# Float32 rows for two blocks of the weight fold, joint group scores, accumulating transfers last in the local sums, and a new instruction order

## The chip, the cores and the metric

The kernel runs on one core of a Trainium2 chip. The metric is the device time of that core in microseconds, the median of three runs. TensorE (PE) multiplies matrices, VectorE (DVE) and ScalarE (ACT) work element by element, GpSimd (POOL) and SyncE (SP) mostly start transfers.

## The reference

Attention over q, k, v of 8 batches x 8 heads x 576 positions x 64, the sum of two parts, and then a gated feed-forward block over all 4608 tokens:

```python
q_d = q.reshape(B, H, Sd, 4, D).mean(axis=3)          # k_d, v_d alike: pooled by 4
out_up = np.repeat(sm_attn(q_d, k_d, v_d), 4, axis=2)  # pooled attention, repeated
mask = np.abs(pos[:, None] - pos[None, :]) < 4         # each position and 3 to either side
out_local = softmax(where(mask, q @ k.T / 8, -1e9)) @ v
x = (out_up + out_local)  ->  (4608, 512)
h = ((x @ w1) * (x @ w2)) @ w3;   out = h @ w_out      # 512->1024, 1024->1024, 1024->512
```

The weights arrive as 64-bit words. The output is float32.

## The kernel before

**Stages.** The two last weight matrices are multiplied first (the fold: w3 @ w_out, 1024 x 512, kept in `wphl`). Then each chunk `c` of 384 tokens (twelve of them, `moe`) runs eight "gates" steps (x @ w1 and x @ w2, product in `a`, split into `gh` and `gl`) and "down" products with the folded weight. A product in full precision is three float32r matmuls (function `three`, lines 312 to 314): each operand is split into a high and a low part, and high x high, high x low, low x high are added up in PSUM.

**The fold.** Its inner dimension is cut into eight blocks `j`, its rows into eight blocks `m` (`mq` 0 has m = 0 to 3, `mq` 1 the others), so 64 products, each three matmuls of 512 columns. For a block `j`, a row block of w_out and one of w3 are loaded as 64-bit words (`words`), put together into float32 on ACT and DVE (`rebase`, `low`, and `join` on line 359), and split (`parted`): ACT casts the high part (line 371), DVE subtracts it for the low part (line 375). Four raw buffers hold loads (`early_raw`). Before the products PE runs 20 matmuls of zeros (`warm`, line 412).

**Attention.** In batches 0 and 1 (`PB`) the local part is computed by PE: `pooled_sums` loads q (`q4`, one transfer for each pair of heads) and k (`k4`), turns q (`qn`, line 672) and adds up four positions each for the pooled attention (`qks`); `group_scores` makes scores of 16 positions against 18 (line 769), two of its calls (`qd` 0 and 1) for each of six units; DVE adds the mask `band` and takes maxima, ACT exponentiates. In batches 2 to 7 (18 units, `unit`) DVE and ACT compute it: seven products q x shifted k, their sums, a softmax over seven, and seven products `pv` with the shifted v. These are added into `xl` in a fixed sequence, of which the places in `dma_add` are accumulating transfers started by POOL (line 958) and the others are additions on DVE (line 960). DVE then transposes (line 964), adds the pooled part (line 971), ACT and DVE split the result into `xh` and `xl` of the chunk (line 978). `quad` is the pooled attention.

**What sets the order.** All steps are tasks of a planner. A table of numbers (`ORDER`) gives each engine its tasks in a fixed sequence; every engine works strictly in that sequence and waits for semaphores where data or a buffer is not there yet. Buffer counts stand in `BUFS`.

Of the kernel before, what the change touches and what calls it, by code (L numbers as in the profile page):

```python
# [20 lines left out]
FAC = 4  # L21
# [31 lines left out]
            g=2, o=2, ab=2, acc=1, ps=3, p=1, pt=1, oup=2, vs=1, qks=1, x=2, s=3, gs=3, q4=2, k4=2, qn=2, vw=4, se=4, pte=1, xf=1)  # L53


SHARE = dict(qk_pool=(), qk_act=(2, 4), av_act=(3, 5), dma_add=(2, 4, 6))
TOKENS = 2
WARM = 20
# [94 lines left out]
    ),  # L153
    Pool=(
# [3 lines left out]
    ),  # L158
    SP=(
# [1064 lines left out]
```

## Time and profile before

| | |
|---|---|
| median of 3 runs | 749.47 us (749.1 to 751.64) |
| profiled execution, span | 747.4 us |
| its own time outside the span | not recorded; the median stands 2.1 us over the span |
| PE busy | 729.4 us (98%) |
| DVE busy | 617.8 us (83%), from 200 to 600 us 95% |
| ACT busy | 544.3 us (73%) |
| POOL busy | 108.2 us (14%) |
| chain that ended last | PE 96%, DVE 2%, DMA 1% |

A matmul's record is longer than its share of time, since the next one starts before it ends; spacing from start to start is what counts. A float32 matmul is two records, one of float32r is one.

### The profile page before, as it was taken

Reading aid. Unit: us, or ns where it says so; the run is one execution under the profiler, and the core shown is the slowest. Engines: PE = TensorE matmul, PEld = TensorE weight load, DVE = VectorE, ACT = ScalarE, POOL = GpSimd, SP = SyncE. Lnnn points to the kernel's source line nnn. Section 1 sums busy time; section 2 is a strip of 40 time slices with the busy share of each in tenths; the row PEclk is TensorE's granted clock in tenths of the full one; section 3 lists DMA queues with packets and bytes.
Section 4 is the critical chain, followed back from the end, with each engine's and each line's share of the span. In section 5 each row is a group of like instructions: output and inputs, shape, how many; then the busy total and the mean of one; then the engine's idle time right before and its main releaser. Section 6 shows DMA issues by size and latency. Waiting matters only on the chain.

```text
span 747.4 us, 15049 instructions
## 1 busy us (share of the span) xinstructions
PE 729.4 (98%) x5352; PEld 658.2 (88%) x5352; DVE 617.8 (83%) x1088; ACT 544.3 (73%) x2157; POOL 108.2 (14%) x139
## 2 busy tenths in 40 slices
PE   4999999999999999999999999999999999999997
PEld 3677888789998989999898998999899999999996
DVE  6988996557999999989999998999989988885212
ACT  5999878566897878778878886877887875853211
POOL 2020002210112210212222110221120110010000
PEclk9999999999999999999999999999999999999999
DMA  8998765746767877396577674668666354233101
GB/s 257 322 261 262 236 204 105 131 84 194 151 143 175 167 171 189 61 241 165 89 168 220 120 184 150 100 197 176 141 145 164 63 152 127 63 66 56 43 0 43
DMA packets 51999, 111.91 MB, mean 150 GB/s; under 512 B 5060, under 2 KB 19396, under 8 KB 51924
## 3 DMA queue, kind: packets, MB, share of 16 engines
q0 software_dynamic: 14592, 38.94, 30.9%
q1 hardware_dynamic: 37044, 71.74, 29.0%
q8 instruction: 42, 0.69, 0.4%
q10 hardware_dynamic: 288, 0.27, 0.1%
q14 instruction: 33, 0.27, 0.1%
HBM read 80.26 MB, written 9.44 MB: 120 GB/s over the span
## 4 chain that ended last, share of the span: by engine, by line
PE 96%; DVE 2%; DMA 1%; issue 0%; ACT 0%; SPq 0%
PE pab L312 19%; PE pab L314 18%; PE pab L313 18%; PE acc L312 9%; PE acc L313 9%; PE acc L314 9%; PE o_ps L553 2%; PE accw L312 2%; PE s_ps L592 2%; PE t_ps L631 2%; PE accw L313 2%; PE accw L314 2%; PE se_ps L769 1%; PE oe_ps L812 1%; PE te_ps L739 1%; DMA q<-in_qk_dram 1%
## 5 line engine op out<-in xcount | busy, mean ns | idle before, releaser
L942 ACT ACTIVATE pv<-kv,s 128x64 f32<-128x64 f32 x432 | 115.3, 338 | 15.2 <-DVE s L919 8.9
L894 ACT ACTIVATE junk<-pr 128x64 f32<-128x64 f32 x432 | 110.2, 255 | 17.3 <-DVE pr L884 8.0
L884 DVE TENSOR_TENSOR pr<-q_t,kv 128x768 f32<-128x768 f32 x126 | 115.8, 950 | 0.6 <-ACT junk L894 0.3
L312 PE MATMUL acc<-wphl,gh 128*128 128x512 f32 x288 | 113.6, 395 | 0.0
L314 PE MATMUL acc<-wphl,gl 128*128 128x512 f32 x288 | 112.9, 392 | 0.0
L313 PE MATMUL acc<-wphl,gh 128*128 128x512 f32 x288 | 112.8, 392 | 0.0
L958 POOL DMA_DIRECT2D xl<-pv x54 | 46.5, 862 | 370.2 <-DVE xl L960 271.3
L1047 DVE TENSOR_TENSOR a<-pab,a 128x384 f32<-128x384 f32 x96 | 53.1, 553 | 45.1 <-PE pab L314 35.2
L1045 ACT COPY a<-pab 128x384 f32<-128x384 f32 x96 | 45.3, 471 | 60.4 <-PE pab L314 56.3
L897 DVE TENSOR_REDUCE s<-pr 128x12 f32<-128x768 f32 x90 | 83.8, 946 | 0.4
L894 ACT ACTIVATION_READ_ACCUMULATOR junk<-pr 128x1 f32 x432 | 81.1, 188 | 0.0
L1052 ACT CAST gh<-a 128x384 fp32r<-128x384 f32 x96 | 48.9, 510 | 38.5 <-PE acc L313 27.5
L1054 DVE TENSOR_TENSOR gl<-a,gh 128x384 fp32r<-128x384 f32 x96 | 52.7, 552 | 26.8 <-ACT gh L1052 26.5
L950 DVE TENSOR_TENSOR pv<-kv,s 128x768 f32<-128x768 f32 x72 | 67.7, 951 | 0.4
L312 PE MATMUL pab<-xh,w1a 128*128 128x384 f32 x192 | 65.7, 342 | 0.0
L312 PE MATMUL pab<-xh,w2a 128*128 128x384 f32 x192 | 65.4, 340 | 0.0
L312 PE MATMUL pab<-xh,wo 128*128 128x384 f32 x192 | 65.3, 340 | 0.0
L312 PE MATMUL pab<-xh,wb 128*128 128x384 f32 x192 | 65.2, 339 | 0.0
L314 PE MATMUL pab<-xh,wo 128*128 128x384 f32 x192 | 64.5, 336 | 0.0
L314 PE MATMUL pab<-xh,wb 128*128 128x384 f32 x192 | 64.5, 336 | 0.0
L314 PE MATMUL pab<-xh,w1a 128*128 128x384 f32 x192 | 64.5, 336 | 0.0
L313 PE MATMUL pab<-xl,wo 128*128 128x384 f32 x192 | 64.5, 336 | 0.0
(126 smaller groups left out, 1766.6 us busy)
## 6 DMA issues: line engine op xcount, KB each, us to landing
xl<-pv POOLq DMA_DIRECT2D x54, 384.0 KB, 4.2
raw<-in_w_dram SPq DMA_DIRECT2D x32, 512.0 KB, 5.3
qks<-in_qk_dram POOLq DMA_DIRECT2D x18, 576.0 KB, 7.3
kv<-in_kw_dram SPq DMA_DIRECT2D x18, 576.0 KB, 4.1
kv<-in_vw_dram SPq DMA_DIRECT2D x18, 576.0 KB, 5.5
q_t<-in_q_dram SPq DMA_DIRECT2D x18, 384.0 KB, 3.3
vs<-in_v_dram POOLq DMA_DIRECT2D x24, 256.0 KB, 5.7
out_dram<-o_sb SPq DMA_DIRECT2D x23, 256.0 KB, 2.8
```

The costliest lines, as they stand in the source:

```text
L312: nc.tensor.matmul(out_ps, lhsT=lh, rhs=rh, start=first, stop=False)
L313: nc.tensor.matmul(out_ps, lhsT=lh, rhs=rl, start=False, stop=False)
L314: nc.tensor.matmul(out_ps, lhsT=ll, rhs=rh, start=False, stop=last)
L884: (nc.gpsimd if o in share["qk_pool"] else nc.vector).tensor_tensor(out=T[o], in0=T["q"], in1=T["k"][:, o * D:o * D + nq].rearrange("p (t ...
L894: nc.scalar.activation(out=junk, in_=T[o][:, t], func=AF.Copy, accum_out=T["s"][:, t, o:o + 1])
L897: reds.append(add("DVE", dve_us(nq), lambda o=o: nc.vector.tensor_reduce(out=T["s"][:, :, o], in_=T[o], op=ALU.add, axis=AX.X), [tp], uses ...
L942: nc.scalar.mul(out=T["pv", o][:, tt], in_=T["v"][:, (tt + o) * D:(tt + o + 1) * D], mul=T["s"][:, tt, o:o + 1])
L950: nc.vector.tensor_tensor(out=T["pv", o], in0=T["v"][:, o * D:o * D + nq].rearrange("p (t d) -> p t d", d=D), in1=T["s"][:, :, o].unsqueez ...
L958: t = add("Pool", 0.9, lambda o=o: nc.gpsimd.dma_start(out=T["x"], in_=T["pv", o], accum_op=ALU.add), [t, tm], uses=[hx, h], late=dma_us(1 ...
L1047: tg = add("DVE", dve_us(CT), lambda f=f: nc.vector.tensor_tensor(out=straight(T["a", f]), in0=turned(T["p", 1, f]), in1=straight(T["a", f ...
L1052: nc.scalar.copy(out=T["gh", f], in_=T["a", f])
L1054: tl = add("DVE", dve_us(CT), lambda f=f: nc.vector.tensor_tensor(out=T["gl", f], in0=T["a", f], in1=T["gh", f].bitcast(F32), op=ALU.subtr ...
```

## The change

- Blocks `j` = 0 and 1 of the fold (`WHOLE`) are no longer split: the joined float32 words are multiplied as they are, one float32 matmul of 512 columns in place of three float32r ones. The joined w_out rows are put into buffers of the ring `oup`.
- `warm` has 33 matmuls, was 20.
- `pooled_sums` loads q of two pairs of heads in one transfer, with one buffer (was two), turns it in one instruction and adds in instructions twice as wide.
- `group_scores` makes both halves in one call: 24 matmuls in a row, and each mask, maximum and normalising instruction twice as wide.
- For batch 0 the pooled softmax is normalised by DVE, two wide instructions in place of four to six on ACT (`NORM_DVE`).
- The mask `band` is copied by GpSimd, was VectorE.
- The local sums: places 1, 2, 3 are added by DVE and 4, 5, 6 by accumulating transfers; before, transfers had places 2, 4, 6.
- `ORDER` is new on all engines.

```diff
-            ... gs=3, q4=2, k4=2, qn=2, vw=4, se=4, pte=1, xf=1)
+            ... gs=3, q4=1, k4=2, qn=2, vw=4, se=2, pte=1, xf=1)
-SHARE = dict(qk_pool=(), qk_act=(2, 4), av_act=(3, 5), dma_add=(2, 4, 6))
+SHARE = dict(qk_pool=(), qk_act=(2, 4), av_act=(3, 5), dma_add=(4, 5, 6))
-WARM = 20
+WARM = 33
 ORDER = dict(
     DVE=(
-        "1 0 71 5 4 73 72 74 8 22-23 2 75 3 76 24 6 25 7 78 9-10 77 80 12 82 11 15 83 79 13 84 16-17 81 14 85 89 87 90 86 88 29-32 36 92 "
...
+NORM_DVE = (0,)
+WHOLE = (0, 1)
...
+    def whole(src, parts, place, take=()):
+        T, ld, tx, h = words(src, place, list(take), "early", parts)
+        early.append(tx)
+        return T, [tx], h
...
+        if j in WHOLE:
+            T, wo_ready[j], wo_held[j] = whole(wout[j].unsqueeze(1), 1, lambda: work.tile([128, KT * SD], F32, name="oup", bufs=BUFS["oup"])[:, :DM], [R["oup"]])
+            wo_whole[j] = T
+            return
...
-                three(accs[m], T["h"][:, cs], T["l"][:, cs], wo[0][:, j], wo_low[:, j], j == 0, j == NF - 1)
+                if j in WHOLE:
+                    nc.tensor.matmul(accs[m], lhsT=T["x"][:, cs], rhs=wo_whole[j]["x"], start=j == 0, stop=j == NF - 1)
+                else:
+                    three(accs[m], T["h"][:, cs], T["l"][:, cs], wo[0][:, j], wo_low[:, j], j == 0, j == NF - 1)
...
-        for par, i in slots:
+        if b in NORM_DVE:
+            for par in range(2):
+                no.append(add("DVE", ..., lambda par=par: nc.vector.tensor_tensor(out=T["of"][par][:, :, :width[par]], ...
+        for par, i in slots if b not in NORM_DVE else ():
...
-                    x["q"] = pools["pep"].tile([128, FAC, SD], F32, name="q4", bufs=BUFS["q4"])
+                x["q"] = pools["pep"].tile([128, FAC, 2, SD], F32, name="q4", bufs=BUFS["q4"])
...
-        quads = [group_scores(b, j, qd, starts) for qd in range(2)]
+        U, hs, no = group_scores(b, j, starts)
...
+            for qd in range(2):
+                for g, (q0, k0) in enumerate(starts):
...
+                            nc.tensor.matmul(U["s", par][w * GQ:w * GQ + GQ, qd, g], ...
-                nc.vector.tensor_copy(out=band[half * GQ:half * GQ + GQ, i], in_=both[...])
+                nc.gpsimd.tensor_copy(out=band[rows, i], in_=both[...])
```

**PE at the start.** `accw` are the fold's accumulators, `still` the zeros, `k` and `qn` the operands of the group scores, `wo`, `wphl` and `w` the split weights. Before:

```order
L769 MATMUL se_ps<-k_153,qn 64x72 x12
L412 MATMUL accw_197<-still 128x128 x20
L312 MATMUL accw_197<-wo,w_178 128x512
L313 MATMUL accw_197<-wphl,w_178 128x512
L314 MATMUL accw_197<-wo,w_178 128x512
L312 MATMUL accw_199<-wo,w_178 128x512
```

Now, where `oup` and `wx` are the joined words of w_out and w3:

```order
L429 MATMUL accw_145<-still 128x128 x33
L456 MATMUL accw_147<-oup,wx 128x512
L456 MATMUL accw_146<-oup,wx 128x512
L456 MATMUL accw_145<-oup,wx 128x512
L456 MATMUL accw<-oup,wx 128x512
L456 MATMUL accw_146<-oup,wx 128x512
L456 MATMUL accw_145<-oup,wx 128x512
L456 MATMUL accw_147<-oup,wx 128x512
L456 MATMUL accw<-oup,wx 128x512
L779 MATMUL se_ps<-k_191,qn 64x72 x12
L779 MATMUL se_ps<-k_193,qn 64x72 x12
L316 MATMUL accw_147<-wo,w_285 128x512
```

The zeros moved ahead of everything, the eight float32 products follow them, and the scores and the first split product (`j` = 2) come after.

**DVE at the start.** Names as above; `q_...` and `k_...` are the loads of `pooled_sums`. Before, from its first instruction that waits for a load:

```order
L683 TENSOR_TENSOR qks<-q_145 128x144
L672 COPY qn<-q_145 128x576
L359 SCALAR_TENSOR_TENSOR wx<-wx,raw 128x512
L683 TENSOR_TENSOR qks<-q_151 128x144
L672 COPY qn<-q_151 128x576
L359 SCALAR_TENSOR_TENSOR wx<-wx,raw 128x512
L1149 COPY band<-xh_97 64x72 x8
L375 TENSOR_TENSOR wphl<-wx,wo 128x512
L375 TENSOR_TENSOR w_178<-wx,w_178 128x512
```

Now:

```order
L363 SCALAR_TENSOR_TENSOR oup<-oup,raw 128x512
L705 TENSOR_TENSOR qks<-q_181 128x288
L705 TENSOR_TENSOR qks<-qks,q_181 128x288 x2
L695 COPY qn<-q_181 128x1152
L360 TENSOR_SCALAR raw<-raw 128x512
L363 SCALAR_TENSOR_TENSOR wx<-wx,raw 128x512
L363 SCALAR_TENSOR_TENSOR oup<-oup,raw 128x512
L705 TENSOR_TENSOR qks<-k_193 128x288
L363 SCALAR_TENSOR_TENSOR wx<-wx,raw 128x512
L705 TENSOR_TENSOR qks<-q_211 128x288
```

The copies of `band` and the first two subtractions are gone; the joins of both whole blocks stand early, the second w3 join behind the first addition of the last k load.

**DVE at the last unit.** `xl<-xl,pv` is the unit's last addition, the transpose `xt<-xl` needs all transfers into it, and `xl_...<-xt,xh_...` completes the last chunk. Before:

```order
L960 TENSOR_TENSOR xl<-xl,pv 128x768
L1054 TENSOR_TENSOR gl<-a,gh 128x384
L978 TENSOR_TENSOR xl_8484<-xt,xh_8483 128x4x192
L1047 TENSOR_TENSOR a<-pab,a 128x384
L1054 TENSOR_TENSOR gl<-a,gh 128x384
L964 STREAM_TRANSPOSE xt<-xl 128x768
L1054 TENSOR_TENSOR gl<-a,gh 128x384
L971 TENSOR_TENSOR xt<-xt,oup 128x768
L978 TENSOR_TENSOR xl_8484<-xt,xh_8483 128x4x192
```

Now:

```order
L971 TENSOR_TENSOR xl<-xl,pv 128x768
L1058 TENSOR_TENSOR a<-pab,a 128x384
L1065 TENSOR_TENSOR gl<-a,gh 128x384
L1058 TENSOR_TENSOR a<-pab,a 128x384
L1065 TENSOR_TENSOR gl<-a,gh 128x384
L961 TENSOR_TENSOR pv<-kv,s_81 128x768
L1058 TENSOR_TENSOR a<-pab,a 128x384
L1065 TENSOR_TENSOR gl<-a,gh 128x384
L989 TENSOR_TENSOR xl_8364<-xt,xh_8363 128x4x192
L975 STREAM_TRANSPOSE xt<-xl 128x768
L982 TENSOR_TENSOR xt<-xt,oup 128x768
L989 TENSOR_TENSOR xl_8364<-xt,xh_8363 128x4x192
```

Between the last addition and the transpose stood one `a`, now there stand three, and a product `pv` whose transfer the transpose needs too.

## Rows read from the trace of the kernel before

**Rows 1.** The page, busy us, share and instructions of PE and PEld.

```profile
PE 729.4 (98%) x5352; PEld 658.2 (88%) x5352; DVE 617.8 (83%) x1088; ACT 544.3 (73%) x2157; POOL 108.2 (14%) x139
```

**Rows 2.** Waits of PE: engine, line, for whom, us, times, longest.

```profile
PE se_ps L769 <- DVE se L780: 0.7, 1, 0.7
PE accw L314 <- DVE w L375: 0.7, 1, 0.7
```

**Rows 3.** Timeline of PE: start us, us, engine, line, out<-in, times, idle before.

```profile
11.10 1.03 PE L769 MATMUL se_ps<-k,qn 64*64 64x72 f32 x24 [11.10 <-DMA k<-in_qk_dram]
12.06 7.17 PE L412 MATMUL accw<-still 128*128 128x128 f32 x40
19.00 0.48 PE L312 MATMUL accw<-wo,w 128*128 128x512 f32 x1
...
28.96 0.50 PE L312 MATMUL accw<-wo,w 128*128 128x512 f32 x1
...
741.82 0.39 PE L314 MATMUL acc<-wphl,gl 128*128 128x512 f32 x1
```

**Rows 4.** Timeline of PE, warm matmuls: those ending after 12.9, those ending after 17.57.

```profile
12.65 4.69 PE L412 MATMUL accw<-still 128*128 128x128 f32 x21
...
17.40 1.84 PE L412 MATMUL accw<-still 128*128 128x128 f32 x15
```

**Rows 5.** Timeline of PE, a score group and products around it.

```profile
30.55 0.97 PE L769 MATMUL se_ps<-k,qn 64*64 64x72 f32 x24
31.45 0.50 PE L312 MATMUL accw<-wo,w 128*128 128x512 f32 x1
...
32.26 0.40 PE L312 MATMUL accw<-wo,w 128*128 128x512 f32 x1
...
32.96 0.39 PE L312 MATMUL accw<-wo,w 128*128 128x512 f32 x1
```

**Rows 6.** Timeline of all engines at the start: first users of loads, and the mask.

```profile
4.07 0.31 DVE L683 TENSOR_TENSOR qks<-q 128x144 f32<-128x144 f32 x1 [2.88 <-DMA q<-in_qk_dram]
...
4.57 1.31 POOL L1146 TENSOR_SCALAR_AFFINE_SELECT xh<-xh 128x72 f32<-128x72 f32 x3
5.66 0.65 ACT L352 ACTIVATE raw<-raw 128x512 int32<-128x512 uint16 x1 [2.88 <-DMA raw<-in_wout_dram]
...
8.41 0.66 ACT L344 ACTIVATE wx<-raw 128x512 f32<-128x512 f32 x1 [1.56 <-DMA raw<-in_w_dram]
...
10.80 1.04 DVE L1149 COPY band<-xh 64x72 f32<-64x72 f32 x8
...
13.82 0.67 ACT L344 ACTIVATE wx<-raw 128x512 f32<-128x512 f32 x1 [0.82 <-DMA raw<-in_w_dram]
```

**Rows 7.** Groups of DVE, shapes apart: times, busy us, mean ns, idle before.

```profile
L789 DVE TENSOR_REDUCE emx<-se 128x6 f32<-128x432 f32 x12 | 7.2, 600 | 0.2
...
L700 DVE TENSOR_TENSOR qks<-qks,k 128x288 f32<-128x288 f32 x8 | 3.6, 451 | 0.1
```

**Rows 8.** Timeline of DVE: two turned copies, and the fold's block `j` = 7.

```profile
19.71 1.25 DVE L672 COPY qn<-q 128x576 f32<-128x576 f32 x2
...
43.70 0.69 DVE L375 TENSOR_TENSOR w<-wx,w 128x512 fp32r<-128x512 f32 x1 [0.47 <-ACT w L371]
44.31 0.42 DVE L356 TENSOR_SCALAR raw<-raw 128x512 int32<-128x512 int32 x1
```

**Rows 9.** The page, transfers: out<-in, queue, times, size, us to landing.

```profile
xl<-pv POOLq DMA_DIRECT2D x54, 384.0 KB, 4.2
```

**Rows 10.** Timeline at the last unit: last addition, transpose, split, first use.

```profile
681.75 0.95 DVE L960 TENSOR_TENSOR xl<-xl,pv 128x768 f32<-128x768 f32 x1
...
687.22 0.97 DVE L964 STREAM_TRANSPOSE xt<-xl 128x768 f32<-128x768 f32 x1
...
691.14 0.96 DVE L978 TENSOR_TENSOR xl<-xt,xh 128x768 fp32r<-128x768 f32 x1 [0.90 <-ACT xh L977]
...
692.55 0.34 PE L313 MATMUL pab<-xl,w1a 128*128 128x384 f32 x1
```

More of the change, by code (lines that the diff above doesn't have):

```diff
@@ L445, in product @@
             else:
-                t = add("PE", 3 * mm_us(DM), prod, deps, uses=[h, held[m]])
+                t = add("PE", 3 * mm_us(DM), prod, deps, uses=[h, held[m]] + wh)
             last[m] = t
@@ L458, in fold @@
             for j in range(NF):
-                if not mq:
+                if not mq and j not in WHOLE:
                     out_weight(j)
@@ L658, in pooled_sums @@
         for qd in range(2):
-            fours[b][qd] = {}
-            tq = hn = None
-            for w in range(2):
-                x = {}
-                def load_q(qd=qd, w=w, x=x):
-                    x["q"] = pools["pep"].tile([128, FAC, SD], F32, name="q4", bufs=BUFS["q4"])
-                    nc.sync.dma_start(out=x["q"], in_=qk4[b, :, :, 0, 2 * qd + w].rearrange("f p s -> p f s"))
-                lq4, hq4 = add("SP", 0.5, load_q, take=[R["q4"]], late=dma_us(128 * 2304))
-                def turn(qd=qd, w=w, x=x):
-                    if w == 0:
-                        fours[b][qd][0] = pools["pep"].tile([128, 2, SD, FAC], F32, name="qn", bufs=BUFS["qn"])
-                    nc.vector.tensor_copy(out=fours[b][qd][0][:, w], in_=x["q"].rearrange("p f s -> p s f"))
-                if w == 0:
-                    tq, hn = add("DVE", dve_us(4 * SD), turn, [lq4], take=[R["qn"]], uses=[hq4])
-                else:
-                    tq = add("DVE", dve_us(4 * SD), turn, [lq4, tq], uses=[hq4, hn])
-                t = lq4
+            x = fours[b][qd] = {}
@@ new lines, in turn @@
+            def turn(x=x):
+                x["n"] = pools["pep"].tile([128, 2, SD, FAC], F32, name="qn", bufs=BUFS["qn"])
+                nc.vector.tensor_copy(out=x["n"], in_=x["q"].rearrange("p f w s -> p w s f"))
+            lq4, hq4 = add("SP", 0.5, load_q, take=[R["q4"]], late=dma_us(128 * 4608))
+            tq, hn = add("DVE", dve_us(8 * SD), turn, [lq4], take=[R["qn"]], uses=[hq4])
+            lk4, hk4 = add("SP", 0.5, load_k, take=[R["k4"]], late=dma_us(128 * 4608))
+            for i, (nm, t, h4) in enumerate((("q", lq4, hq4), ("k", lk4, hk4))):
@@ L692, in load_k @@
-            def load_k(qd=qd):
-                x = fours[b][qd][1] = pools["pep"].tile([128, FAC, 2, SD], F32, name="k4", bufs=BUFS["k4"])
-                nc.sync.dma_start(out=x.rearrange("p f w s -> p f (w s)"), in_=qk4[b, :, :, 1, 2 * qd:2 * qd + 2].rearrange("f p w s -> p f (w s)"))
-            lk4, hk4 = add("SP", 0.5, load_k, take=[R["k4"]], late=dma_us(128 * 4608))
-            t = lk4
-            for f in range(1, FAC):
-                def total(qd=qd, f=f):
-                    to, x = raws[b][0][:, 1, 2 * qd:2 * qd + 2], fours[b][qd][1]
-                    nc.vector.tensor_tensor(out=to, in0=x[:, 0] if f == 1 else to, in1=x[:, f], op=ALU.add)
-                t = add("DVE", dve_us(2 * SD), total, [t, first], uses=[hk4, hq])
@@ L702, in pooled_sums @@
-            done.append(t)
-            pep.append(lk4)
+            pep.extend([lq4, tq, lk4])
             four_ready[b].append(([tq, lk4], [hn, hk4]))
@@ L756, in group_scores @@
     @plan.named
-    def group_scores(b, j, qd, starts):
+    def group_scores(b, j, starts):
         U = {}
-        l4, h4 = four_ready[b][qd]
+        l4s, h4s = zip(*four_ready[b])
         def score():
             for par in range(2):
-                U["s", par] = ps.tile([128, NG, GK], F32, tag="g", name="se_ps", bufs=BUFS["ps"])
-            for g, (q0, k0) in enumerate(starts):
-                for w in range(2):
-                    for par in range(2):
-                        qs, ks = (fours[b][qd][i][par * D:par * D + D] for i in range(2))
-                        nc.tensor.matmul(U["s", par][w * GQ:w * GQ + GQ, g], lhsT=qs[:, w, q0:q0 + GS].rearrange("p s f -> p (s f)"), rhs=ks[:, :, w, k0:k0 + WS].rearrange("p f s -> p s f"), start=True, stop=True)
-        sc, b0, b1 = add("PE", 2 * NG * mm_us(2 * GK) + SWITCH, score, l4, take=[R["ps"], R["ps"]], uses=h4)
+                U["s", par] = ps.tile([128, 2, NG, GK], F32, tag="g", name="se_ps", bufs=BUFS["ps"])
+            for qd in range(2):
+                for g, (q0, k0) in enumerate(starts):
+                    for w in range(2):
+                        for par in range(2):
+                            qs, ks = (fours[b][qd][i][par * D:par * D + D] for i in "nk")
+                            nc.tensor.matmul(U["s", par][w * GQ:w * GQ + GQ, qd, g], lhsT=qs[:, w, q0:q0 + GS].rearrange("p s f -> p (s f)"), rhs=ks[:, :, w, k0:k0 + WS].rearrange("p f s -> p s f"), start=True, stop=True)
+        sc, b0, b1 = add("PE", 4 * NG * mm_us(2 * GK) + SWITCH, score, sum(l4s, []), take=[R["ps"], R["ps"]], uses=sum(h4s, []))
         pep.append(sc)
@@ L791, in group_scores @@
         ex = []
-        for i in range(2 * NG):
+        for i in range(nb):
             ex.append(add("ACT", act_us(GK, 2), lambda i=i: nc.scalar.activation(out=p3()[:, i], in_=p3()[:, i], func=AF.Exp, bias=U["mx"][:, i:i + 1], scale=1.0 / D ** 0.5, accum_out=U["sm"][:, i:i + 1]), [t], uses=[hs]))
@@ L1097, in tile_attention_moe @@
     rests, sums = {}, {}
+    for j in WHOLE:
+        out_weight(j)
     def scores(n):
@@ L1147, in tile_attention_moe @@
         for half in range(2):
+            rows = slice(half * GQ, half * GQ + GQ)
             for i in range(NG + 1):
-                nc.vector.tensor_copy(out=band[half * GQ:half * GQ + GQ, i], in_=both[half * GQ:half * GQ + GQ, half, 0 if i == 0 else 2 if i == NG else 1])
-    bands.extend([band[:, :NG], band[:, 1:2].to_broadcast([128, NG, WS, FAC]), band[:, 1:]])
+                nc.gpsimd.tensor_copy(out=band[rows, i], in_=both[rows, half, 0 if i == 0 else 2 if i == NG else 1].rearrange("p s f -> p (s f)"))
+    bands.extend([band[:, :NG], band[:, 1:2].to_broadcast([128, NG, GK]), band[:, 1:]])
     with tc.manual_schedule():
```

58 lines of the change are left out of this document (34 added, 24 removed), and 183 rows, old and new, of tables (ACT, DVE, PE, Pool).

## The prediction

> **What bounds the kernel now.** I read the page's busy shares, then the waits of PE, then PE's timeline. PE is busy 98% of the span [rows 1]. It waits for the k load until 11.10 us, and behind that only for two waits of 0.7 us [rows 2, 3], the second of them in the fold's first block. From 28.96 us to the end of the last matmul, 741.82 + 0.39 = 742.2, it never waits again. So the time is: when PE gets going, plus PE's own work, plus new waits of PE, plus what lies behind its last matmul (747.4 − 742.2 = 5.2 us to the span's end, and 2.1 us from the profiled span to the median of 749.47). VectorE, though 95% busy from 200 to 600 us, hands over each chunk in time; at the last one with 692.55 − 692.10 = 0.45 us to spare [rows 10]. A gain must therefore come from the start or from PE's work, and a loss from VectorE being late.
>
> **PE's work.** A product of three float32r matmuls takes 0.70 us from one to the next [rows 5]. In blocks 0 and 1, 16 products become one float32 matmul of 512 columns each. The trace has no such shape; the nearest row is the zeros, 128 columns, also float32: at the high clock 15 records take 1.84 us up to the next product's start at 19.00, and the middle spacing is 0.11, so the two records of one matmul take 0.21 to 0.22 us [rows 4]. Four times the columns give 0.85 to 0.89; I take 0.86, since a fixed part per record would shrink. That adds 16 x 0.16 = 2.6 us. Bounds: no cost if float32 rows run like three float32r passes (0), and 0.93 − 0.70 = 0.23 each if as four (3.7).
>
> That second bound is also a page's: the Trainium skill, FP8 and Floating Point Precision, section TensorE Precision Notes, gives true FP32 four passes through the array. By it a product is 4/3 x 0.70 = 0.93 us, an estimate, and the time 1.1 us longer; the two records of a float32 matmul here neither prove nor exclude it.
>
> A score group holds PE 0.90 us from its start to the next product's start, and the products beside it are pushed by some 0.1 each way, 1.1 in all [rows 5]. Two groups in one call run their matmuls on and save one entry and exit: estimated 1.85 for both, 0.33 saved, in five places behind the start 1.6 us. Sum of PE's work: +2.6 − 1.6 = +1.0 us.
>
> **PE's start.** The zeros are now first and depend only on a memset, so they begin near 1.2 us. Before, the low clock level (1.2 GHz) held from the first matmuls at 11.10 or 12.06 to about 17.1, 0.22 us per record with 0.11 after it [rows 3, 4], so 5 to 6 us; the same from 1.2 us on would end by 7.3 and let the rest run fast: 66 records at 0.22 and then 0.11 end near 11.0 to 11.5. What follows needs block 0, so its loads decide. I order the loads by bytes. Before, first users show 288 KB landed by 4.07, 800 by 5.66, 1312 by 8.41, 2176 by 11.10 (k, PE's first wait) and 3200 by 13.82 [rows 3, 6]. In the new order a pair of q's (576 KB), two rows of w_out, two of w3 (512 each), two k (576 each) and a second q pair reach 576, 1088, 1600, 2112, 2624, 3200, 3776 and 4352 KB, on the same curve 5.0, 7.2, 9.3, 10.9, 12.2, 13.8, 15.35 and 16.9 us. Block 0's w3 row at 10.9, ACT's 0.66 [rows 6], and VectorE's join behind the turned copy of q (1.25, [rows 8]) and its own shift give the first product at **12.9 us**, where the first split product stood at 19.00 [rows 3]. The four products of block 0 that come first last 3.4 us, to 16.3; block 1's join is queued on VectorE behind the addition for the k of 15.35 and ends near 16.5, so the four of block 1 follow with hardly a wait.
>
> **Where the head start goes.** The head start is 6.1 us, but PE reaches VectorE. VectorE can't start the long row of joins and subtractions of blocks 2 to 7 before the last q at 16.9. From there to the subtraction of block 7, which before ended at 43.70 + 0.69 = 44.39, it has: 12 joins and 12 subtractions at 0.60 from start to start (44.31 − 43.70, [rows 8]) 14.4; 8 partial sums, the narrow ones 0.31 [rows 6], the 288 wide 0.45 [rows 7], taken as 0.37 together, 3.0; a turned copy 1.2; four mask additions near 0.52, 2.1, and their maxima, one joint one near 1.0 and two at half of that or less, 1.7 (432 elements took 0.60, [rows 7]); four shifts near 0.34 in spacing, 1.4; 0.2 small ones: 24.0. With 1.0 for waits on ACT it is done at **41.9**, 2.5 us before the old time. The copies of the mask, 1.04 [rows 6], are gone from VectorE. On POOL eight copies cost no more than its affine selects, 1.31 / 3 = 0.44 each [rows 6], done by about 9.4 and needed beyond 20: nothing. Only at some five times that would the first mask addition wait.
>
> So behind 41.9 everything on PE that needs VectorE stands 2.5 us earlier: the last maximum, two wide normalising products in place of ACT's narrow ones (2.3), the pooled group's transposes near 45.0. The end is counted from there. Before, the work from 28.96 to 742.2 was 713.25 without waits, with the eight products and three score groups ahead of it 5.6 + 2.9 = 721.7; now +1.0 = 722.7. Of that, the new order has ahead of them: eight float32 products 6.9, two joint score groups 3.7, the pooled scores 0.85 (an estimate: eight matmuls of 144 columns at some 0.11), 23 split products 16.1, and 0.6 of the transposes themselves: 28.1. The rest, 694.6, ends at **739.6**, against 742.2: **−2.6 us**. Without a wait PE would end at 12.9 + 722.7 = 735.6; the other 4.0 us are waits of PE for VectorE, all before 45.
>
> **Costed at nothing.** The single q buffer: the next q waits for the turned copy near 11.7, but its transfer stands behind both k's anyway. Normalising on VectorE: 2.3 us there, less on ACT, which is 73% busy. Local sums: the three transfers, each 4.2 us to landing [rows 9], now follow one another, some 13 us with the waits between, ahead of a transpose that had one behind the last addition. In 16 of 18 units the new order puts 16 to 27 us of other VectorE work between; POOL, which starts them, has little else. In the last two units it is 11 and 4.5 us of work, but four and three `a` stand there, and each waits for PE's gates, some 4 us apart. If that cover is gone, the transpose and everything queued behind it on VectorE wait; that is rival C.
>
> **Rivals.** A, *no change*, about 749.5: the 2.5 us at block 7 are eaten. VectorE's sum of 25.0 us has terms without a row (1.0 for waits, shapes twice as wide), and loads 2 us later than the curve move everything alike. For it: VectorE has no slack from 16.9 to 41.9. Against it: the loads are the same bytes. Products at the upper bound of 0.93 us (748.0) end on its side too.
>
> B, *faster still*, 745.5: the loads run at the rate of the last stretch, 1024 KB in 2.72 us [rows 3, 6], from 5.66 on, not at the slower 186 KB/us between 5.66 and 8.41. Then q is there at 15.5 instead of 16.9 and all is 1.4 earlier. For it: the slow stretch may have been a pause in issuing. Against: nothing in the change removes such a pause.
>
> C, *slower*, 755.2: at the last unit the transfers are uncovered. 13.2 − 4.5 = 8.7 us late, less the 0.45 of slack [rows 10] is PE waiting 8.3 us at the last chunk: 746.9 + 8.3. It decides if the three `a` between take less than 8.7 us longer than their own work. For it: VectorE may run ahead or behind; three transfers queue on one engine. Against: PE's own gates, four to six us per pair of `a`, pace them, and VectorE at the earlier chunks had several us in hand.
>
> D, *slower*, 753.7: TensorE's clock falls again in the pause of 1.4 to 1.9 us between the zeros and the first product. Eight float32 products would then take twice 0.86, 6.8 us more. In before, a wait of 0.7 us left the spacing of products behind it as it was [rows 2, 5], and no longer pause inside the run is to be seen there.
>
> A page speaks for D: the Trainium skill, TensorE: Matmul & The Clock Gate, section Why this matters for your kernels, says that idle gaps between bursts take the clock back. By that rule the time would be 753.7 if a pause as short as this one counts; the trace has only the 0.7 us wait to set against it.
>
> That the change doesn't do what it says is excluded by the order of instructions: all eight edits are there.
>
> **How the numbers follow.** One profile can't tell under 0.3% (2.25 us): faster is below 747.2, slower above 751.7. The forecast, **746.9**, stands close to that edge; its case, with 2 us of spread either way, has 0.60: 0.38 below 747.2 and 0.22 above it. A has 0.14, B 0.11, C 0.09, D 0.03, and 0.03 is for VectorE late at a middle chunk by 5 us or more. So faster 0.38 + 0.11 = 0.49, same 0.22 + 0.14 = 0.36, slower 0.09 + 0.03 + 0.03 = 0.15. The range reaches from 743.8 (B at 745.5, with most of the 2.6 us for float32 products not spent) to 751.7, the end of A, and leaves out C, D and the middle chunk, 0.15.
>
> **What would show it.** In the profile after: zeros from about 1.2 us, the first float32 product at 12.9, spaced 0.86 (0.93: four passes; twice that: D). The last q's first addition at 16.9, block 7's subtraction ending at 41.9. PE's waits on VectorE several, some 3 to 5 us together, all before 45 us, and none behind. The transfers of the local sums still at 4.2 us. Last matmul ending at 739.6. A wait of PE at the last chunk would be C; loads 2 us late, or block 7 at 44, would be A; a wait in the middle on `xl` or `gl` would be the case that I gave 0.03.

## The result: 755.62 us, slower by 0.8%

The changed kernel takes 755.62 us (median of four runs, 754.05 to 758.2), the kernel before 749.33 beside it: a ratio of 1.0082, 95% interval 1.0057 to 1.0106. The forecast was 746.9 and its range ended at 751.7, so the change is slower where I gave that 0.15. The profiled execution took 757.13 us with a span of 755.3.

The first line of the page shows TensorE (PE) and the other engines of the changed kernel, as [rows 1] did:

```profile
PE 738.1 (98%) x5362; PEld 657.9 (87%) x5362; DVE 605.2 (80%) x1020; ACT 536.6 (71%) x2141; POOL 109.4 (14%) x147
```

VectorE (DVE) does less than before, 605.2 against 617.8 us, and PE is still busy 98% of a span that is 7.9 us longer. So the loss is again to be looked for in PE's start, its work and its waits. PE's timeline of the changed kernel (columns as in [rows 3]):

```profile
1.13 9.04 PE L429 MATMUL accw<-still 128*128 128x128 f32 x66 [1.13 <-DVE still L298]
12.34 7.13 PE L456 MATMUL accw<-oup,wx 128*128 128x512 f32 x16 [2.17 <-DVE wx L363]
...
43.86 1.07 PE L655 MATMUL t_ps<-ident,pexp 128*128 128x128 f32 x6
...
62.87 0.50 PE L318 MATMUL accw<-wo,w 128*128 128x512 f32 x1 [1.62 <-DVE w L380]
...
79.38 0.32 PE L823 MATMUL oe_ps<-pte,v_w 72*32 72x64 f32 x8 [0.81 <-DMA v_w<-in_v_dram]
80.28 1.32 PE L823 MATMUL oe_ps<-pte,v_w 72*32 72x64 f32 x80 [0.58 <-DMA v_w<-in_v_dram]
...
87.01 0.44 PE L316 MATMUL pab<-xh,w1a 128*128 128x384 f32 x1 [1.25 <-issue]
...
355.98 0.45 PE L316 MATMUL pab<-xh,wo 128*128 128x384 f32 x1 [1.06 <-ACT a L1056]
...
749.52 0.39 PE L318 MATMUL acc<-wphl,gl 128*128 128x512 f32 x1
```

The first product stands at 12.34 us, where the first split product was at 19.00 [rows 3], and the transposes `t_ps` stand at 43.86: this is the start that the prediction asked for, even a little earlier. Behind it the list has what the prediction ruled out: waits between 60 and 88 us, and one at 356. The first gates (`pab`) start at 87.01; in the kernel before they start at 83.65:

```profile
83.65 0.44 PE L312 MATMUL pab<-xh,w1a 128*128 128x384 f32 x1
```

So a lead near 45 us had become a lag of 3.4 us at the first gates, and the last matmul ends at 749.52 + 0.39 = 749.9, 7.7 us behind that of before (742.2).

**One measure for all kernels.** Since the orders differ, the same instant means different work done. I use a *projected end*: the start of PE's next matmul, plus all matmuls that PE still has to do, each at the mean spacing that its pair of shapes has in the profile of before (pairs that before lacks, from the changed kernel, the few with one case or two by their likes; stops over 0.25 us left out, zeros counted as nothing). A projected end rises only where PE loses time, and falls where it runs with fewer small stops than the mean. PE's whole work by this is 721.7 us before and 722.6 after. No view of the profile prints this measure, it is worked out from the starts of all PE records. What is taken for the pairs with few cases moves all levels alike by up to 2.8 us, but the differences between the kernels by no more than 0.6. The column "end" is the start of the last matmul.

```
projected end of PE (us) at time   45     65     75     84     89     300    400    end
before                           741.9  741.6  741.9  742.1  742.0  743.8  743.4  741.8
changed kernel                   738.6  740.7  741.0  743.0  744.5  747.0  749.3  749.5
changed kernel, run again        739.4  742.0  744.8  747.0  748.6  752.4  752.6  752.8
```

At 45 us the changed kernel is 3.3 us ahead. From 45 to 89 it loses 5.9 us (before: 0.1), from 89 to 300 another 2.5 (before 1.8). Behind 300 it loses 2.5 more where before gains 2.0. Together −3.3 + 5.8 + 0.7 + 4.5 = 7.7 us, the lag of the last matmul. Each row is one execution. That of before took 749.47 us and those of the changed kernel 757.13 and, run again, 760.38, both above its median.

### The profile page after: what moved, and what is told of

Its sections match the earlier page's. It is cut to its first block, busy times and chain, and to the rows that moved or that the text cites. A ratio compares the mean times of both kernels' runs of the same rounds, so it can differ in the third digit from the quotient of the medians.

```text
span 755.3 us, 14948 instructions
## 1 busy us (share of the span) xinstructions
PE 738.1 (98%) x5362; PEld 657.9 (87%) x5362; DVE 605.2 (80%) x1020; ACT 536.6 (71%) x2141; POOL 109.4 (14%) x147
## 4 chain that ended last, share of the span: by engine, by line
PE 67%; DVE 14%; DMA 11%; ACT 4%; issue 2%; POOL 0%; SPq 0%; DVEq 0%; ACTq 0%; POOLq 0%
PE pab L316 13%; PE pab L318 13%; PE pab L317 13%; PE acc L316 7%; PE acc L317 7%; PE acc L318 7%; DMA xl<-pv 3%; DVE pr L895 3%; DMA vl<-in_v_dram 2%; DMA vs<-in_v_dram 2%; PE o_ps L574 2%; DVE pv L961 1%; DVE s L908 1%; DMA q_t<-in_q_dram 1%; ACT pv L953 1%
## 5 line engine op out<-in xcount | busy, mean ns | idle before, releaser
L953 ACT ACTIVATE pv<-kv,s 128x64 f32<-128x64 f32 x432 | 116.7, 337 | 16.9 <-DVE s L930 11.2
L318 PEld LDWEIGHTS acc<-wphl,gl 128*128 128x128 f32 x288 | 54.0, 188 | 12.2 <-DVE gl L1065 0.3
```

Of the source, the lines that this page charges most:

```text
L318: nc.tensor.matmul(out_ps, lhsT=ll, rhs=rh, start=False, stop=last)
L953: nc.scalar.mul(out=T["pv", o][:, tt], in_=T["v"][:, (tt + o) * D:(tt + o + 1) * D], mul=T["s"][:, tt, o:o + 1])
```

## Experiments

All are timed against the kernel before, whose medians beside them were 749.3 to 749.9. "Old" is the order of before, "new" that of the changed kernel. An edit of the order is told in words or by its rows, since its numbers tell nothing.

**1 and 2. Front of one order, back of the other.** The first has the new order up to the first gates and the old one behind it, with the places of the transferred sums of before; the second the reverse.

```diff
-SHARE = dict(qk_pool=(), qk_act=(2, 4), av_act=(3, 5), dma_add=(4, 5, 6))
+SHARE = dict(qk_pool=(), qk_act=(2, 4), av_act=(3, 5), dma_add=(2, 4, 6))
```

> The changed kernel up to the first gates matmul (same loads, zeros, float32 blocks, joint groups, same sequence), and behind it the sequence of before with transfers at places 2, 4, 6. In the profile of the changed kernel the first gates matmul starts at 87.01 us, before at 83.65 (3.4 later), and from there to PE's last matmul it is 662.9 us against 658.6 (4.3 longer). Theory 'two losses' (a late front and waits of ACT on accumulating transfers behind it): this kernel pays the front's alone, 749.3 + 3.4 = 752.7 us. Rival 'all from the front, the later waits only follow from it': 755.6. Rival 'all from the local sums': 749 or below.

> The kernel before up to the first gates matmul, and behind it the sequence of the changed kernel with transfers at places 4, 5, 6 (blocks of the fold, groups and loads as before). Theory 'two losses': it pays those behind the front alone, 749.3 + 4.3 = 753.6 us. Rival 'all from the front': 749.5. Rival 'all from the local sums': 755.6.

Measured 761.26 us (1.0152 [1.0135, 1.0169]) and 766.35 (1.0227 [1.0204, 1.025]). All theories missed: both are slower than either parent. The stretch behind the joint costs: from 89 to 300 us the projected ends rise by 10.1 and 14.1 us. PE's waits in the first, 88 to 300 us (engine, line, for whom: us, times, longest):

```profile
PE te_ps L741 <- DVE se L800: 5.0, 3, 3.0
```

VectorE comes to the scores late here. That the rows behind the joint were placed for an older front is the likely reason, but it was not shown. What can be read is behind 300 us, far from the joint: the old back falls by 2.0 (755.1 to 753.1), as in before; the new back rises by 1.6 (756.0 to 757.6). Each back has its own places of the sums with it.

**3. A fourth buffer for the values that are summed.** ACT writes a product into a `pv` buffer (L953) that an accumulating transfer may still be reading. With four buffers in place of three it should not wait; room for the fourth comes from `junk`, which now shares the tile of the zeros.

```diff
-BUFS = dict(pr=3, pv=3, xl=2, xt=1, q=1, kv=3, w3=3, early_raw=4, early_wx=3, late_raw=3, late_wx=2, a=2,
+BUFS = dict(pr=3, pv=4, xl=2, xt=1, q=1, kv=3, w3=3, early_raw=4, early_wx=3, late_raw=3, late_wx=2, a=2,
-    junk = wpool.tile([128, D], F32, name="junk")
+    junk = still[:, :D]
```

> The changed kernel with four buffers for the products with shifted v (was three; the room comes from a scratch tile that shares the zeros' place). In the profile of the changed kernel ACT waits 3.24 us at 346.4 for a transfer to give back such a buffer (the third of three in a row, 8.8 us from issue to landing), and PE behind it 0.30 and 1.06 us for ACT. Theory 'transfers in a row hold the buffers': these waits go, PE's waits behind 300 us fall from 1.9 to under 0.5, and the time falls by 2 to 4 us, to 752 to 753.6. Rival 'VectorE or ACT is late on its own there': within 1 us of 755.6.

Measured 755.64 us (1.0082 [1.0053, 1.0112]): no gain. In the changed kernel ACT's timeline has the wait that stands ahead of PE's stop at 355.98, and the chain of waits has the three transfers it stood behind:

```profile
346.43 2.02 ACT L953 ACTIVATE pv<-kv,s 128x64 f32<-128x64 f32 x8 [3.24 <-DMA xl<-pv]
```

```profile
322.92 9.65 DMA xl<-pv
333.10 3.96 DMA xl<-pv
337.62 8.78 DMA xl<-pv
```

Two of the three took 9.7 and 8.8 us, not 4.2. With four buffers this wait is gone, but the timelines of ACT and PE there show another late load, and PE stops for ACT again:

```profile
359.79 0.62 ACT L559 COPY vl<-vl 16x512 f32<-16x512 f32 x1 [3.06 <-DMA vl<-in_v_dram]
361.12 0.45 PE L317 MATMUL pab<-xh,wb 128*128 128x384 f32 x1 [0.70 <-ACT a L1057]
```

**4 and 5. The zeros.** 70 of them, so that PE reaches block 0 later, and 20, so that a longer pause lies ahead of the first product.

```diff
-WARM = 33
+WARM = 70
```

> The changed kernel with 70 zero matmuls in place of 33: at the measured 0.21 us each at the high clock they end near 18.1 us, so the first float32 product starts some 5.8 us later than its 12.34. Theory 'the head start is worth nothing, since loads, ACT and VectorE bound everything up to the first gates matmul': within 1 us of 755.6. Rival 'the head start is carried to the end': 761.4.

> The changed kernel with 20 zero matmuls in place of 33: they end near 7.3 us, and PE has nothing to do until the first float32 product at 12.3. Theory 'a pause of 5 us takes the high clock away': the eight first products are spaced 1.76 us instead of 0.88 for at least some of them, and the time is 2 to 7 us longer, 757.6 to 762.6. Rival 'the clock stays at its high level': spacing 0.88, time within 1 us of 755.6.

70 zeros: 758.2 us (1.0098 [1.0078, 1.0119]), between the two theories. PE's projected end at 45 us is 742.3 instead of 738.6, and the median is 2.6 us longer. (The two intervals overlap, so the 2.6 is not certain, and how much of a later start reaches the end stays open: in the profile, of the slowest of six executions, the wait for `v_w` is gone but that for `w` is 2.0 us instead of 1.6, and the granted clock behind it is 0.67 in 65 to 75 us, see experiment 14.) 20 zeros: 756.17 us (1.0078 [1.0062, 1.0095]), not to be told from the changed kernel. PE's timeline of it:

```profile
11.84 7.13 PE L456 MATMUL accw<-oup,wx 128*128 128x512 f32 x16 [3.35 <-DVE wx L363]
...
23.60 0.51 PE L318 MATMUL accw<-wo,w 128*128 128x512 f32 x1
...
24.34 0.63 PE L317 MATMUL accw<-wphl,w 128*128 128x512 f32 x1
```

After a pause of 3.35 us the float32 products keep their duration (7.13 us for 16 records, as after 2.17 us). Split matmuls some 12 us later are slower (0.63 instead of 0.40), which adds less than 1 us to them. The pause is not what sets this apart: the changed kernel run again, whose pause was 0.46 us, has the same granted clock there. Busy time of the engines, then the granted clock (PEclk), the DMA share and GB/s, from 22 to 28 us, 20 zeros first, then the changed kernel run again:

```profile
22.00:28.00 6.00, 5.81 (x61) 4.11 (x62) 5.76 (x11) 5.52 (x10) 0.00 (x0) 0.72 0.81 262
22.00:28.00 6.00, 5.81 (x61) 4.11 (x61) 5.76 (x11) 5.55 (x11) 0.00 (x0) 0.72 0.81 283
```

Ahead of this stretch PE waits 1.1 to 1.25 us near 21 us in twelve of the profiles with the new front. Eight of them show 0.72 from 22 to 28 us and four 1.00, the first profile of the changed kernel among these.

**6. Only the sums at their old places**, in an order that is new otherwise.

```diff
-SHARE = dict(qk_pool=(), qk_act=(2, 4), av_act=(3, 5), dma_add=(4, 5, 6))
+SHARE = dict(qk_pool=(), qk_act=(2, 4), av_act=(3, 5), dma_add=(2, 4, 6))
```

> The changed kernel with the local sums' transfers back at places 2, 4, 6 and the additions at 1, 3, 5; each unit's middle additions are moved back in VectorE's sequence to where a transfer of 4 to 5 us has landed, everything else keeps the new sequence. From 210 us on the changed kernel loses some 5 us to the kernel before, at places where a transfer of three in a row took 6 to 9.7 us. Theory 'three in a row leave no slack': from 210 us on PE loses no more than before does, the time falls by 3 to 5 us, to 751 to 753. Rival 'the new sequence is too tight there whatever the places': within 1 us of 755.6 or slower.

Measured 823.93 us (1.0989 [1.0949, 1.1029]). The first theory missed; the rival's "or slower" has the direction, but neither foresaw 68 us. VectorE's waits from 240 us on:

```profile
DVE pv L961 <- DMA xl<-pv: 47.2, 15, 6.1
```

An order built for sums of one kind, with only the middle additions moved, has no cover for the other: here VectorE must wait until the transfer has read its buffer. Places and order can't be taken apart in this way; what the run does show is the price of an uncovered transfer, 3 us at a time.

**7. The copy of the first `vl` later.** In the changed kernel VectorE stands still ahead of PE's stop at 62.87. Its timeline:

```profile
57.98 0.68 DVE L363 SCALAR_TENSOR_TENSOR wx<-wx,raw 128x512 int32<-128x512 int32 x1
61.68 0.42 DVE L556 COPY vl<-vl 16x512 f32<-16x512 f32 x1 [3.02 <-DMA vl<-in_v_dram]
62.13 0.69 DVE L380 TENSOR_TENSOR w<-wx,w 128x512 fp32r<-128x512 f32 x1
```

A small copy waits 3.02 us for its load, and the subtraction for PE's next block, whose inputs are there, is queued behind it. In before the same copy ran later, without a wait that the timeline shows:

```profile
64.49 0.42 DVE L535 COPY vl<-vl 16x512 f32<-16x512 f32 x1
```

The edit takes it behind the subtraction, a shift and a reciprocal; the order on VectorE:

```diff
 L363 SCALAR_TENSOR_TENSOR wx<-wx,raw 128x512
+L380 TENSOR_TENSOR w_665<-wx,w_665 128x512
+L360 TENSOR_SCALAR raw<-raw 128x512
+L806 RECIPROCAL esm<-esm 128x12
 L556 COPY vl<-vl 16x512
-L380 TENSOR_TENSOR w_665<-wx,w_665 128x512
-L360 TENSOR_SCALAR raw<-raw 128x512
-L806 RECIPROCAL esm<-esm 128x12
```

> The changed kernel with one instruction of VectorE moved back by three places: the copy of vl (16 x 512), at which VectorE waited 3.02 us for a load until 61.7 us, now stands behind the subtraction that PE waited for (1.62 us). Theory 'VectorE's wait at this load is carried to the first gates matmul': PE's wait there falls to 0.5 or less, the first gates matmul starts at 85.8 instead of 87.0 and the time falls by 1 to 3 us, to 752.6 to 754.6. Rival 'the loads of v_w set the first gates matmul': it stays at 87 and the time within 0.7 us of 755.6.

Measured 756.62 us (1.0088 [1.0064, 1.0112]): nothing gained. PE's stop for `w` is gone, and the next one took over half of it. PE's waits of this kernel, 45 to 88 us:

```profile
PE oe_ps L823 <- DMA v_w<-in_v_dram: 2.2, 2, 1.8
```

They were 1.4 us for `v_w` in the changed kernel. The first of these waits ends at 79.37 us here and at 79.38 there: the load is as late as before, and PE, which comes earlier, waits longer. Behind it the granted clock is 0.85 from 75 to 84 us, where the changed kernel's first profile has 1.00.

**8. That, and the `v_w` loads ahead of the next batch's `vs` and `vl`.** The order on SyncE, which starts them:

```diff
+L731 DMA v_w<-in_v_dram 36x1x512 x2
+L731 DMA v_w<-in_v_dram 72x1x512
 L538 DMA vs<-in_v_dram 128x512
 L539 DMA vl<-in_v_dram 16x512
-L731 DMA v_w<-in_v_dram 36x1x512 x2
-L731 DMA v_w<-in_v_dram 72x1x512
```

> The same, and on SP two loads of v_w for the second group unit moved ahead of the load of vs and vl for the next batch. PE waited 1.4 us for these two loads at 79.4 and 80.3 us. Theory 'both loads set the front': the first gates matmul starts at 84.5 or before and the time falls by 2.5 to 4 us against the changed kernel, to 751.6 to 753. Rival 'something else (ACT, VectorE) is late next': no more than new_vl_later gains.

Measured 754.33 us (1.0061 [1.0049, 1.0074]), 1.3 us below the changed kernel and less than the 2.5 to 4 of the theory; the intervals overlap. In its profile the waits for `vl` and `v_w` are nearly gone (PE's waits, 45 to 88 us), and the first gates start at 83.24, earlier than in before (waits, then the timeline):

```profile
PE pab L316 <- DVE wphl L475: 0.8, 2, 0.6
PE oe_ps L823 <- DMA v_w<-in_v_dram: 0.4, 1, 0.4
```

```profile
83.24 0.45 PE L316 MATMUL pab<-xh,w1a 128*128 128x384 f32 x1 [0.59 <-DVE wphl L475]
```

So both waits in the front have the causes named. What they are worth in the median stays uncertain: this profile is of the fastest of five executions (752.73 us), and the granted clock did not fall in its front. Its projected ends (below) then rise from 741.2 at 89 us to 745.1, where those of before end as they stood: with the front mended, what lies behind is what is left.

**9 and 10. Behind 89 us: are it the transfers, or their buffers?** On top of experiment 8, transfers that carry 64 of the 768 columns (the rest is not added, so the sums are incomplete), and, in the other kernel, the fourth `pv` buffer.

```diff
-nc.gpsimd.dma_start(out=T["x"], in_=T["pv", o], accum_op=ALU.add)
+nc.gpsimd.dma_start(out=T["x"][:, :1], in_=T["pv", o][:, :1], accum_op=ALU.add)
```

> As new_vl_vw, but each accumulating transfer of the local sums moves 64 of its 768 columns (a twelfth of the bytes; the other columns of that addition are left out of the result). Sequence, places and buffers are unchanged. Theory 'the transfers in a row are what is late behind 88 us': with short transfers PE loses behind 88 us no more than before does, which takes 3 to 4 us away: 750 to 751.5 against 754.3 for new_vl_vw. Rival 'the new sequence itself is tight, whatever the transfers take': within 1 us of 754.3.

> As new_vl_vw, with the fourth buffer for the products of new_pv4. With three buffers alone new_pv4 took ACT's wait for a buffer away and lost 1.5 us at an accumulating load of vl 14 us later. Theory 'buffers held by transfers': 1 to 2 us below new_vl_vw, 752.3 to 753.3. Rival 'any late transfer on POOL's queue, not the buffers': within 0.7 us of 754.3.

Light transfers: 753.41 us (1.0058 [1.0042, 1.0074]); four buffers: 754.94 (1.0074 [1.006, 1.0088]). The light transfers take 2.4 us to landing in the median, from 2.1 to 7.7; three of the 54 take over 6 us, as many as in before, against thirteen in experiment 8. Neither can be told from experiment 8, so the length of the three transfers in a row, the part of the change that I had feared most, is not the main cause, nor are their buffers.

**11 to 13. Joints elsewhere.** With the front of experiment 8 and the old order from about 235 us on; the new order up to 235 us and the old behind it, with the sums' places changing at the same unit; and the reverse.

```diff
-i in share["dma_add"]
+i in (share["dma_add"] if n < 9 else (2, 4, 6))
```

> As new_vl_vw up to the fifth gates step of chunk 2 (near 235 us), and from there the sequence of before, with places 2, 4, 6 for the units that start behind it. Theory 'the later sequence with its sums costs 2 to 4 us behind 235 us': the time is 750 to 752 (VectorE is some 4 us of work behind the sequence of before at the cut, part of which may show as a wait). Rival 'the loss has arisen by 235 us': within 1 us of 754.3.

> new_vl_vw up to the fifth gates step of chunk 2 (near 235 us), the sequence of before behind it, with places 2, 4, 6 for the units that start there. At the cut the two sequences have done the same work on VectorE and PE to within 1 us. Theory 'the new sequence with its sums costs 2 to 2.5 us behind 235 us': 751.5 to 752.5, against 754.3 for new_vl_vw. Rival 'the loss has arisen by 235 us': within 0.8 us of 754.3.

> The reverse: the kernel before up to the same point, behind it the new sequence with places 4, 5, 6 for the units that start there. Theory 'the new sequence with its sums costs 2 to 2.5 us behind 235 us': 751.4 to 752.2. Rival 'nothing behind 235 us': within 0.8 us of 749.4.

The first took 845.86 us (1.1294 [1.1266, 1.1322]). I had put its order together wrongly, each transpose right behind the transfer that it reads. VectorE's waits from 240 us on show what that costs:

```profile
DVE xt L970 <- DMA xl<-pv: 55.3, 14, 5.9
```

The other two took 765.95 us (1.0207 [1.0192, 1.0222]) and 761.99 (1.0162 [1.0137, 1.0186]). Again the stretch at the joint spoils the total: between 89 and 300 us the projected ends rise by 15.9 and 11.3, with these waits of PE (first kernel 250 to 300 us, then the second):

```profile
PE o_ps L569 <- DMA vs<-in_v_dram: 4.9, 1, 4.9
PE pab L311 <- ACT a L1051: 3.1, 1, 3.1
```

```profile
PE pab L316 <- DVE a L1051: 6.7, 1, 6.7
```

The waits are not all of it: behind them the granted clock falls. The engines' busy time and, third from the right, the clock, in the first kernel and in the second:

```profile
275.00:300.00 25.00, 17.00 (x132) 14.10 (x129) 14.11 (x19) 13.85 (x63) 4.33 (x5) 0.80 0.73 160
265.00:280.00 15.00, 8.26 (x32) 7.60 (x31) 10.95 (x21) 3.36 (x13) 3.39 (x4) 0.77 0.63 138
```

And again the stretch behind tells the orders apart: the old one falls by 2.1 behind 300 us, the new one rises by 2.0.

**14. The changed kernel again**, to see which of its waits belong to it and which to one execution.

> The changed kernel once more, unchanged. Theory 'the waits that carry the loss are fixed by the sequence': PE's waits at the copy of vl (1.6 us) and at the loads of v_w (1.4 us together) are there again, each within 1 us, and the time is 755.6 within 1. Rival 'they fall elsewhere in every execution': one of the two is under 0.3 us.

Measured 755.57 us (1.0081 [1.0057, 1.0104]). PE's waits from 45 us on, of an execution of 760.38 us:

```profile
PE accw L318 <- DVE w L380: 1.9, 1, 1.9
PE oe_ps L823 <- DMA v_w<-in_v_dram: 1.8, 1, 1.8
...
PE pab L316 <- issue: 0.6, 1, 0.6
```

The same three waits stand at the same places, so they are set by the order, and their sizes differ by up to 0.65 us. But in this execution something came on top that the first profile does not have: behind the wait for `w` the granted clock fell, and again behind that for `v_w`. The engines' busy time, then the clock, the DMA share and GB/s; the changed kernel's first profile, then twice the one run again:

```profile
65.00:75.00 10.00, 10.00 (x177) 7.98 (x162) 8.80 (x19) 8.83 (x20) 0.00 (x0) 1.00 0.81 273
65.00:75.00 10.00, 10.00 (x95) 6.62 (x94) 6.84 (x13) 6.30 (x17) 0.00 (x0) 0.68 0.62 207
84.00:89.00 5.00, 4.58 (x94) 3.62 (x98) 2.83 (x7) 2.50 (x5) 1.66 (x2) 0.66 0.96 323
```

From 66 to 71 us the clock stands at 0.50, the lower of its two levels (1.2 and 2.4 GHz). PE is busy all the time from 65 to 75 us in both, yet the projected end rises by 2.8 us in this one and by 0.3 in the first: more than the wait itself cost. Seven profiles have this wait for `w`, of 1.6 to 2.1 us; in four of them the clock of the ten microseconds behind is 0.67 to 0.70, in three 1.00. What decides it, these runs do not show. Over the ten executions of the changed kernel the mean granted clock was 0.990 to 1.000 (middle 0.994), over 44 of the kernel before 0.996 to 1.000 (middle 0.998). How much of the 0.8% this makes was not separated: the first profile shows 1.00 in every stretch behind the zeros, and that execution still took 757.13 us.

No kernel of these beats the one before.

Where the projected ends rise in the kernels that read cleanly, and in the joined ones behind 300 us:

```
projected end (us)            at 45      89     300     end   behind 300
before                        741.9   742.0   743.8   741.8     -2.0
changed kernel                738.6   744.5   747.0   749.5     +2.5
changed kernel, run again     739.4   748.6   752.4   752.8     +0.4
8: vl and v_w mended          738.2   741.2   745.0   745.1     +0.1
9: 8, light transfers         738.8   741.8   744.6   744.6      0.0
10: 8, four buffers           738.1   743.7   746.3   747.3     +1.0
1: new, then old                                                -2.0
12: new to 235 us, then old                                     -2.1
2: old, then new                                                +1.6
13: old to 235 us, then new                                     +2.0
```

Three profiles with the old back fall by 2.0 or 2.1, whatever lies ahead of it. All with the new back stay or rise, by 0.0 to 2.5; the two executions of the changed kernel alone lie 2.1 apart, so the kernels with the new back can't be ranked by this. The granted clock is 1.00 there in all of these profiles up to 700 us. The loss has no large wait. PE's waits of the changed kernel from 300 us on, all that its profile lists (for before it lists none):

```profile
PE pab L316 <- ACT a L1056: 1.6, 2, 1.1
PE acc L316 <- ACT gh L1063: 0.3, 1, 0.3
```

Counted from record to record, over the middle spacing of each pair of shapes, PE loses 10.2 us behind 300 us in before, 14.5 in the changed kernel and 12.1 in experiment 8. Of the 4.3 us between the first two, three stops of over 0.25 us make 2.4, more stops of 0.1 to 0.25 us 0.9 (33 instead of 26), and 0.9 is spread over some 2,600 matmuls at under 0.03 us each.

## Why the prediction was wrong, step by step

**Right: the start.** The float32 products began at 12.34 us for 12.9, the last q's first addition at 16.04 for 16.9, block 7's subtraction ended at 41.18 + 0.68 = 41.86 for 41.9, and the transposes stood at 43.86 for 45.0. VectorE's sum of 25 us, which rival A doubted, held: 25.8 were needed. The zeros, too, came out earlier: they ended at 10.17 us for 11.0 to 11.5, since their records are 0.23 us apart only up to some 4 us, where the prediction carried the 5 to 6 us of before over to the new start, up to 7.3. The loads were 0.9 us ahead of the curve, part of the way to rival B (whose rate, taken from 5.66 us on as it says, gives the last q at 15.1 and not at 15.5). The rows, the zeros up to 4.1 us and from 4.2 to 10 us first:

```profile
1.13 3.24 PE L429 MATMUL accw<-still 128*128 128x128 f32 x14 [1.13 <-DVE still L298]
3.85 6.32 PE L429 MATMUL accw<-still 128*128 128x128 f32 x54
...
16.04 0.46 DVE L705 TENSOR_TENSOR qks<-q 128x288 f32<-128x288 f32 x1 [0.59 <-DMA q<-in_qk_dram]
...
41.18 0.68 DVE L380 TENSOR_TENSOR w<-wx,w 128x512 fp32r<-128x512 f32 x1
```

**Right: PE's work.** 722.6 us for 722.7, though all shapes that before has too stand in that sum at their spacings of before, so only the new ones are tested by it. A float32 product takes (19.41 − 12.34) / 8 = 0.88 us with what lies between, for 0.86; a joint score group is 26.82 − 25.15 = 1.67 us ahead of the next product, where 1.85 was estimated for its whole cost. The page of the Trainium skill that the prediction weighed (FP8 and Floating Point Precision, TensorE Precision Notes, four passes for true FP32) gave 0.93: the trace stands between three passes (0.70) and four, nearer to four. PE's timeline of a joint group:

```profile
25.15 1.74 PE L779 MATMUL se_ps<-k,qn 64*64 64x72 f32 x48
26.82 0.50 PE L316 MATMUL accw<-wo,w 128*128 128x512 f32 x1
```

**Right: rivals that did not come.** POOL's eight copies of the band took 1.62 us and delayed nothing. The products behind the pause of 2.17 us ran at 0.88 us each, so D did not come where the prediction looked for it; the granted clock fell elsewhere, behind other waits and not in every execution (experiments 5 and 14). The median landing of the sums' transfers is 4.2 us, as in [rows 9], and the last chunk does not wait: the 755.2 of rival C lies near the measured time, but its mechanism is not in the trace.

**Wrong: "all before 45 us, and none behind".** This is the step that failed. The prediction took the 694.6 us of PE's work behind the transposes as running without a stop because in before it ran so. That it did so in before rested on the old order, whose loads were asked for and whose small copies were queued at other places; experiments 7 and 8 show this for two of the waits. The prediction goes through the new order of VectorE up to 45 us and through the transposes behind the sums, and through no other row that waits for a load. The forecast end of PE's last matmul was 739.6; it was 749.9. Of these 10.3 us the projected ends put 5.9 between 45 and 89 us and 5.0 behind; the start, better than forecast, gave back 0.6.

- 45 to 89 us: 1.62 for `w` behind the copy of `vl` (removed by experiment 7), 1.4 for `v_w` (reduced by 8), and 1.25 ahead of the first gates that the profile calls "issue"; the other 1.6 or so are shorter stops. The wait called "issue" stays open: run again it was 0.6, experiment 8 has 0.59 put down to `wphl` there, and experiment 7 has none.
- 45 to 89 us, the clock: the prediction reckoned with it at the pause ahead of the first product alone and put it at nothing behind. In the execution run again it added some 2.5 us between 65 and 75 us.
- Behind 89 us: many stops and few of them long, with every back that has the new order and its places of the sums. Experiments 3, 9 and 10 speak against the buffers and the length of the transfers as the main cause. The prediction had 0.03 for "VectorE late at a middle chunk by 5 us"; what came was PE's small stops. Which moves in the order make them stays open: experiment 6 shows that the sums' places can't be exchanged without the order, and the joints cost more than what was looked for.

**"Costed at nothing" was too kind.** More of the local sums' transfers are late: ten of the 54 took over 6 us, up to 9.7, against three, up to 8.3, in before. ACT's 3.24 us at 346 us came from that. What it is worth is small or nothing as far as the runs tell: lightening the transfers gave 0.9 us, not told apart from nothing.

## What to carry to other kernels

Where the engine that sets the time gets going earlier, its gain is worth only what the next handover lets through: go on reading the new order behind the point where the gain is banked, row by row, for every instruction that waits for a load, and ask what stands behind it on its engine. Here a copy of 0.42 us whose turn came 5.8 us earlier than before (at 58.66 instead of 64.49 us), while its load landed just ahead of 61.68, cost PE 1.6 us, and mending it alone gave nothing, because the next load was as late. Look at the granted clock of the stretch behind a wait as well, and in more than one execution: what follows a wait can cost more than the wait. Parts of two orders, each tuned as a whole, could not be exchanged here: each joint cost some 10 us or more.

## What the hardware showed that I had not expected

- The accumulating transfers of 384 KB differ widely, 3.96 to 9.65 us in three neighbours of experiment 3's chain; carrying a twelfth of the bytes they took 2.4 us in the median, and still up to 7.7.
- In a timeline, a split matmul behind a float32 one seems to take long (52.33 to 52.97 us). That its start is drawn too early is the likely reason, for where one float32 product stands between split ones, the switch shows no cost: from 54.14 to 55.23 us run two float32 records and one split matmul, 1.09 us, and two at (19.41 − 12.34) / 16 = 0.44 and one at 0.23 would be 1.11. PE's timeline of the changed kernel:

```profile
54.14 1.02 PE L456 MATMUL accw<-oup,wx 128*128 128x512 f32 x2
54.59 0.80 PE L316 MATMUL accw<-wo,w 128*128 128x512 f32 x1
55.23 0.40 PE L317 MATMUL accw<-wphl,w 128*128 128x512 f32 x1
```

- Behind the same wait, in the same kernel, the granted clock fell in one execution and not in the other: 1.00 and 0.68 from 65 to 75 us, behind waits of 1.62 and 1.89 us. A pause of 3.35 us (experiment 5) was followed by eight products at the duration that they have behind one of 2.17.
